# Decode attention with a gated output: the output in eight partitions of 112 columns, one store, and wo summed with two folds

## The chip, the core and the metric

The kernel runs on one core of one Trainium2 chip. The core has five engines with instruction queues of their own: TensorE (PE in the profile; its weight loads are listed as PEld), VectorE (DVE), ScalarE (ACT), GpSimd (POOL) and SyncE (SP). They share an on-chip memory of 128 partitions; TensorE writes its results into a second one, PSUM. Sixteen DMA engines move data between it and the device memory; SP and ACT issue transfers to them here. The metric is the device time of one execution in microseconds.

## The reference

The kernel computes one decode step for a batch of two: a layer norm of x, sliding-window attention over the last 2,048 positions of a cache, and a gate from a two-layer network.

```python
# B=2, Sq=1, D=448, Hq=16, Hkv=8, Dh=256, W=2048, Dff=1792; all bfloat16
xn = layernorm(x)                                   # (2, 1, 448)
q = xn @ wq                                         # 448 x 4096
scores = q . k_cache[:, :, Sk-W:, :] * Dh ** -0.5   # 16 heads, two per kv head
o = softmax(scores) . v_cache[:, :, Sk-W:, :]
s = o.reshape(2, 1, 4096) @ wo                      # 4096 x 448
g = silu(relu(xn @ w1) @ w2)
out = x + s * g
```

The caches count for 32 MiB of the loads, the four weight matrices for some 10 MiB more.

## The kernel before, in words

Every operation is put on a list of its engine (`_Prog.op`, `_Prog.dma`) with the operations that it depends on; the lists are emitted in the order in which they were written, with semaphore waits where a dependence crosses engines. So the order of the text is the order of each engine's queue. Nearly all matmuls go through the helper `mm` (line 241) and all transfers through line 35; in the profile they are told apart by their tiles.

SP loads wq, w1, w2, the four K tiles (4 MiB each, one for each batch element and group of four kv heads), then each V tile into the buffer of a K tile once that K tile's scores are done, and last wo in the six parts of `WO_PARTS`, into the buffer that wq had (`wqo`). wo lies with 32 rows j of 448 columns in every partition, so that a part is a range of j.

On TensorE, results of two rows (the batch) are common. To use more of the array, independent matmuls are put into different groups of 32 output columns (`tile_position`): four such groups (i or c times 32) run beside each other, and their results lie in partitions 0, 32, 64 and 96 of a PSUM bank. Where four groups hold partial sums of the same result, a fold adds them up: VectorE copies the bank into on-chip memory (f32), and a matmul with the matrix `f8` of ones sums the partitions 0, 32, 64 and 96.

`do_H` and `do_F` compute the gate early: h, then w2 in four groups into `fbk`, a copy `zc`, a fold into `mbk` in two groups of 224 columns (c = 0, 1, partitions 0 and 32), and the silu on 34 partitions (`ROWS`) by 224 columns (`NCOL`), into `g_sb`. The rows in between are not used.

The middle is the attention: `do_turn` transposes K on VectorE (line 276), `do_S` forms scores into `sbk`, `do_max`, `do_et`, `do_spread` and `do_pt` make the softmax, `do_PV` multiplies with V, `do_out` scales, and `do_turn_out` transposes the result into `at2`, the stationary operand of the wo product: for each j two columns, one of each batch element.

The end is what the change is about. wo's first part of 16 rows is multiplied in four groups into `wbk` (row j in group j mod 4), copied to `wc` (line 451) and folded into `fbk`, in two groups of 224 columns. The other sixteen rows go straight to `fbk` by `direct` (line 453): for each j two matmuls of 224 columns, c = 0 into partitions 0 and 1, c = 1 into 32 and 33. `fill` puts in matmuls whose results nobody reads, between the waits for wo. After the last row VectorE multiplies `fbk` with `g_sb` (line 474) and adds `x_c` (line 476), a copy of x in the same layout, which two small transfers on ACT's queue loaded at the start into memory that POOL had set to zero. Two stores, one on SP's and one on ACT's queue (line 478), write the halves, and each engine waits for its own.

Of the kernel before, what the change touches and what calls it, by code (L numbers as in the profile page):

```python
# [74 lines left out]
def bass_recurrent_scan__sliding_block_cached__dense_activation_relu__decode_kernel(  # L75
# [26 lines left out]
    NCOL = D // 2  # L102
    ROWS = 34
    WO_PARTS = [16, 4, 4, 4, 2, 2]
    WO_TILED = 16

    es = contextlib.ExitStack()
    with es:
# [35 lines left out]
        wc = named("wc", [128, D], F32)  # L144
        ea = named("ea", [128, NCOL], F32)
# [14 lines left out]
        at2 = named("at2", [128, 32 * 2], BF)  # L160
# [19 lines left out]
        p_xc = pr.op(POOL, lambda e: e.memset(x_c[:, :], 0.0))  # L180
        d_xc = [pr.dma(ACTE, x_c[32 * c:32 * c + B, :], A_x[:, 0, NCOL * c:NCOL * c + NCOL], [p_xc]) for c in range(2)]
# [6 lines left out]
        st = {}  # L188
# [3 lines left out]
        for u in range(NU):  # L192
# [7 lines left out]
               for t in (asel, rm, bt, qstat, at2)][-1]  # L200
# [24 lines left out]
        v_f8 = pr.op(DVE, red(f8[:, :], view(ident, 0, [[1, 8], [8, 16]])))  # L225
        v_h2 = pr.op(DVE, red(half2[:, :], view(ident, 0, [[8, 2], [16, 8], [1, 8]]), AX.XY))
# [133 lines left out]
        def do_turn_out(hg):  # L360
            if hg:
                fill(2)
            deps = [st["osb", 2 + hg], v_as, st["mbk"]]
            lo = 64 * hg
            for dq in range(8):
                o = pr.op(PE, mm(mbk[lo:lo + 64, 288:352], asel[:, 7 - dq:71 - dq],
                                 view(o_sb, hg * 2 * DH + 32 * dq, [[DH, B], [1, 32]]),
                                 dq == 0, dq == 7, tile_position=(0, lo)), deps)
                deps = []
            st["at"] = st["mbk"] = pr.op(DVE, lambda e: e.tensor_copy(  # L370
                view(at2, 0, [[1, B], [B, 32]], n=64, p0=lo), view(mbk, 288, [[32, B], [1, 32]], n=64, p0=lo)), [o, p_z])
# [15 lines left out]
        def do_F():  # L387
# [7 lines left out]
            deps = [v, v_f8, st["mbk"]]  # L395
            for c in range(2):
                o = pr.op(PE, mm(mbk[32 * c:32 * c + B, 0:NCOL], f8[:, 0:B], zc[:, NCOL * c:NCOL * c + NCOL],
                                 True, True, tile_position=(0, 32 * c)), deps)
                deps = []
# [46 lines left out]
        for j in range(WO_TILED):  # L446
            i = j % 4
            o = pr.op(PE, mm(wbk[32 * i:32 * i + B, 0:D], at2[:, B * j:B * j + B], wqo[:, j * D:j * D + D],
# [15 lines left out]
        deps = [v_wc]  # L464
        for c in range(2):
            pr.op(PE, mm(fbk[32 * c:32 * c + B, 0:NCOL], f8[:, 0:B], wc[:, NCOL * c:NCOL * c + NCOL], False,
                         tile_position=(0, 32 * c)), deps)
            deps = []
        for j in range(20, 32):
            if j in (20, 24):  # L470
                fill(1)
            m_o = direct(j, [landed.get(j)])
# [4 lines left out]
            out=out_sb[0:ROWS, :], in0=tmp[0:ROWS, :], in1=x_c[0:ROWS, :], op=ALU.add), [v_t] + d_xc)  # L477
# [33 lines left out]
```

## Time and profile before

| | us |
|---|---|
| median of three runs | 110.72 (110.68 to 110.85) |
| the profiled execution | 110.67 |
| its span, first to last instruction | 109.3 |
| DVE busy | 62.2 |
| PE busy | 57.0 |
| the first wo matmul | 102.53 |
| the last wo matmuls | 106.79 to 107.14 |
| product and sum on VectorE | 107.19 to 107.99 |
| both stores issued | 108.02 |

The times inside the span count from its start. Busy times of engines overlap and don't add up to the span. The span does not hold what lies before the first and after the last instruction, 1.3 us in the profiled execution.

### The profile page before, as it was taken

How to read it: one execution, taken by the hardware profiler on the slowest of the kernel's cores; microseconds unless marked ns; L12 is line 12 of the kernel's file. 1: busy time of each engine (PE TensorE's matmuls, PEld its weight loads, DVE VectorE, ACT ScalarE, POOL GpSimd, SP SyncE). 2: the span in 40 equal slices, each digit the busy share in tenths (PEclk: the TensorE clock that was granted, in tenths of full speed). 3: DMA queues.
4: the chain of work that ended last, by engine and by line, in shares of the span. 5: the costliest groups of instructions: out<-in, count | busy, mean ns of one | idle time of the engine just before them, and what ended most of it. 6: DMA issues, size and time to landing. Idle time of an engine off the chain costs nothing.

```text
span 109.3 us, 1081 instructions
## 1 busy us (share of the span) xinstructions
PE 57.0 (52%) x458; PEld 14.5 (13%) x458; DVE 62.2 (57%) x83; ACT 9.1 (8%) x18; POOL 2.1 (2%) x12
## 2 busy tenths in 40 slices
PE   0010559430000079929952994499339555937791
PEld 0000114100000011001100120010023122413230
DVE  2920046445099979999999999930457333004102
ACT  3970000010000000002000200020110000000000
POOL 7000000000000000000000000000000000000000
PEclk9999999985555555999995569958995999999999
DMA  6899999999999999999999999999999899999940
GB/s 168 336 452 397 408 436 501 396 455 438 444 396 455 467 408 396 455 467 408 408 458 444 408 420 467 432 420 402 467 432 420 378 444 420 444 413 410 405 187 1
DMA packets 2616, 44.17 MB, mean 404 GB/s; under 512 B 306, under 2 KB 564, under 8 KB 948
## 3 DMA queue, kind: packets, MB, share of 16 engines
q1 hardware_dynamic: 2596, 44.11, 94.7%
q8 instruction: 3, 0.05, 0.2%
q14 instruction: 1, 0.01, 0.0%
q10 hardware_dynamic: 16, 0.00, 0.0%
HBM read 44.11 MB, written 0.00 MB: 403 GB/s over the span
## 4 chain that ended last, share of the span: by engine, by line
DMA 57%; DVE 28%; PE 7%; SPq 5%; issue 1%
DMA kv<-in_A_k_cache_dram 34%; DVE kv L276 24%; DMA wqo<-in_A_wo_dram 23%; PE sbk L241 7%; SPq L35 5%; DVE q_x L305 1%; DVE rm L293 1%; DVE rm_t L295 0%; DVE bias L299 0%; DVE bt L296 0%; DVE tmp L474 0%; DVE out_sb L476 0%; PE fbk L241 0%
## 5 line engine op out<-in xcount | busy, mean ns | idle before, releaser
L241 PE MATMUL sbk<-kv,qstat 128*8 128x512 bf16 x128 | 29.9, 1086 | 23.9 <-DVE kv L276 23.9
L276 DVE STREAM_TRANSPOSE kv<-kv 128x2048 f32<-128x2048 f32 x16 | 35.6, 2276 | 4.6 <-DMA kv<-in_A_k_cache_dram 4.6
L241 PE MATMUL obk<-kv,pt 128*16 128x512 bf16 x128 | 9.3, 435 | 4.8 <-DVE xg L356 2.4
L241 PEld LDWEIGHTS sbk<-kv,qstat 128*8 128x8 bf16 x128 | 4.0, 107 | 48.4 <-DVE kv L276 30.2
L353 DVE TENSOR_SCALAR o_odd<-obk,rs 128x256 f32<-128x256 f32 x4 | 1.9, 484 | 11.6 <-PE obk L241 11.6
L300 ACT ACTIVATE e_sb<-sbk,bias 128x512 bf16<-128x512 f32 x4 | 2.7, 687 | 52.6 <-DVE bias L299 52.6
L241 PE MATMUL qbk<-wqo,xr 128*4 128x512 bf16 x28 | 3.2, 626 | 5.7 <-DMA wqo<-in_A_wq_dram 5.7
L259 DVE TENSOR_SCALAR q_x<-qbk 128x512 bf16<-128x512 f32 x1 | 0.7, 691 | 8.7 <-PE qbk L241 8.7
L293 DVE TENSOR_REDUCE rm<-sbk 128x1 f32<-128x512 f32 x4 | 2.6, 662 | 4.7 <-PE sbk L241 4.7
L241 PE MATMUL sbk<-kv,ident 128*32 128x512 bf16 x19 | 5.1, 380 | 0.0
L241 PEld LDWEIGHTS obk<-kv,pt 128*16 128x16 bf16 x128 | 3.2, 97 | 10.1 <-issue 5.8
L305 DVE STREAM_TRANSPOSE q_x<-e_sb 128x512 bf16<-128x512 bf16 x4 | 2.8, 691 | 1.7 <-ACT e_sb L300 1.7
L241 PE MATMUL mbk<-ident,xg 2*128 2x2 bf16 x7 | 0.3, 163 | 6.0 <-DVE xg L234 6.0
L322 DVE TENSOR_TENSOR pt<-spk,pmask 128x512 bf16<-128x512 f32 x4 | 2.6, 684 | 0.7 <-PE spk L241 0.7
L241 PE MATMUL qbk<-w_sb,xr 128*2 128x448 bf16 x28 | 2.8, 572 | 0.0
L241 PE MATMUL fbk<-wqo,at 128*2 128x224 bf16 x32 | 2.5, 258 | 0.4 <-DMA wqo<-in_A_wo_dram 0.4
L241 PE MATMUL spk<-q_x,perm 128*32 128x128 bf16 x16 | 0.6, 292 | 3.1 <-DVE q_x L305 3.1
L474 DVE TENSOR_TENSOR tmp<-fbk,g_sb 34x224 f32<-34x224 f32 x1 | 0.4, 383 | 3.1 <-PE fbk L241 3.1
L270 DVE CAST qstat<-mbk 32x256 bf16<-32x256 f32 x4 | 1.7, 421 | 0.7 <-PE mbk L241 0.7
L356 DVE SCALAR_TENSOR_TENSOR xg<-obk,rs,o_odd 128x256 bf16<-128x256 f32 x4 | 1.9, 484 | 0.1
L451 DVE COPY wc<-wbk 128x448 f32<-128x448 f32 x1 | 0.6, 625 | 2.4 <-PE wbk L241 2.4
L241 PEld LDWEIGHTS sbk<-kv,ident 128*32 128x32 bf16 x19 | 1.8, 97 | 1.8
(70 smaller groups left out, 33.1 us busy)
## 6 DMA issues: line engine op xcount, KB each, us to landing
kv<-in_A_k_cache_dram SPq DMA_DIRECT2D x4, 4096.0 KB, 41.3
kv<-in_A_v_cache_dram SPq DMA_DIRECT2D x3, 4096.0 KB, 22.1
kv<-in_A_v_cache_dram SPq DMA_DIRECT2D x2, 2048.0 KB, 18.0
wqo<-in_A_wq_dram SPq DMA_DIRECT2D x1, 3584.0 KB, 11.3
w_sb<-in_B_w_dram SPq DMA_DIRECT2D x2, 1568.0 KB, 16.2
wqo<-in_A_wo_dram SPq DMA_DIRECT2D x1, 1792.0 KB, 23.7
wqo<-in_A_wo_dram SPq DMA_DIRECT2D x3, 448.0 KB, 24.8
wqo<-in_A_wo_dram SPq DMA_DIRECT2D x2, 224.0 KB, 25.5
```

The costliest lines, as they stand in the source:

```text
L35: o = _Op(eng, lambda e: e.dma_start(dst, src), [d for d in deps if d is not None], True)
L241: return lambda e: e.matmul(out_ap, lhsT=lhsT, rhs=rhs, start=start, stop=stop, skip_group_check=True, **kw)
L259: v_q = pr.op(DVE, lambda e: e.tensor_scalar(out=view(q_x, 0, [[256, 8], [128, 2], [1, 32]]), in0=view(qbk, 0, [[64, 8], [1, 2], [2, 32]]) ...
L270: st["q"] = st["mbk"] = pr.op(DVE, lambda e, Q=Q: e.tensor_copy(qstat[32 * Q:32 * Q + 32, 256 * Q:256 * Q + 256], mbk[32 * Q:32 * Q + 32, ...
L276: st["turn", u] = pr.op(DVE, lambda e, n=n: e.transpose(kf[:, 2048 * n:2048 * n + 2048], kf[:, 2048 * n:2048 * n + 2048]), [d_k[u]])
L293: v = pr.op(DVE, lambda e: e.tensor_reduce(out=rm[:, 0:1], in_=sbk[u % 2][:, :], axis=AX.X, op=ALU.max), [last_S[u], p_z, st.get(("rmt", u ...
L300: st["exp", u] = pr.op(ACTE, lambda e: e.activation(e_sb[:, :], sbk[u % 2][:, :], ACT.Exp, bias=bias[:, 0:1], accum_out=ssum[:, u:u + 1]), ...
L305: st["et", u] = pr.op(DVE, lambda e: e.transpose(q_x[:, 512 * u:512 * u + 512], e_sb[:, :]), [st["exp", u], m_qt])
L322: st["pt", u] = pr.op(DVE, lambda e: e.tensor_tensor(out=view(pt[u], 0, [[8, 64], [2, 4], [1, 2]]), in0=view(spk, 128 * u, [[2, 64], [0, 4 ...
L353: v = pr.op(DVE, lambda e: e.tensor_scalar(out=o_odd[:, :], in0=obk[:, DH:2 * DH], scalar1=rs[:, 2 * u + 1:2 * u + 2], scalar2=None, op0=A ...
L356: st["osb", u] = pr.op(DVE, lambda e: e.scalar_tensor_tensor(out=o_sb[:, lo:lo + DH], in0=obk[:, 0:DH], scalar=rs[:, 2 * u:2 * u + 1], in1 ...
L451: v_wc = pr.op(DVE, lambda e: e.tensor_copy(wc[:, :], wbk[:, 0:D]), [o])
```

## The change

The layout of the output changes. It was two pieces (c = 0, 1) of 224 columns, each of two rows at partitions 32c and 32c + 1. It becomes eight adjacent partitions of 112 columns: partition 4b + c holds quarter c of batch element b, which is the order of the output in device memory. x is loaded so by one transfer (`x_c`), and ACT stores the output with one.

A matmul that shall write quarter c into rows 4b + c of eight, and add nothing to the others, takes a stationary operand of eight columns that is zero but for columns c and 4 + c. For this `at2` gets 11 columns for each j, zeros but for columns 3 and 7, and the slice of eight that begins at 3 - c has the two values at c and 4 + c. `fpad` is the same of `f8`, for the gate's fold: four matmuls in sequence into `mbk` rows 0 to 7. These slices have no `tile_position`.

wo comes in five parts (20, 4, 4, 2, 2 rows). Rows 0 to 23 are summed in four groups into `wbk` and folded once, into four groups by quarters in `sbk[1]`; rows 24 to 27 are added there in four groups of 112 columns. VectorE copies that bank (`qc`), and a second fold with `sel8` adds it to `fbk`, rows 0 to 7, in which rows 28 to 31 are summed by padded slices, four matmuls a row. In TensorE's order the second fold stands between rows 29 and 30. Three fills stand ahead of the first fold; the single fills between the later rows are gone. The diff, cut to its core:

```diff
-    NCOL = D // 2
-    ROWS = 34
-    WO_PARTS = [16, 4, 4, 4, 2, 2]
-    WO_TILED = 16
+    NCOL = D // 4
+    ROWS = 8
+    PADW = 11
+    WO_PARTS = [20, 4, 4, 2, 2]
+    WO_TILED = 24
+    WO_QUART = 28
...
-        p_xc = pr.op(POOL, lambda e: e.memset(x_c[:, :], 0.0))
-        d_xc = [pr.dma(ACTE, x_c[32 * c:32 * c + B, :], A_x[:, 0, NCOL * c:NCOL * c + NCOL], [p_xc]) for c in range(2)]
+        d_xc = pr.dma(ACTE, x_c[0:ROWS, :], A_x.rearrange("b s (c n) -> (b s c) n", c=4))
...
-               for t in (asel, rm, bt, qstat, at2)][-1]
+               for t in (fpad, asel, rm, bt, qstat, at2)][-1]
...
+        v_fp = pr.op(DVE, lambda e: e.tensor_copy(view(fpad, 3, [[4, B]]), f8[:, 0:B]), [v_f8, p_z])
+        v_s8 = pr.op(DVE, lambda e: e.tensor_copy(
+            view(sel8, 0, [[4, B], [1, 4]]), view(ident, 0, [[1, B], [32, 4]])), [p_id])
...
-                view(at2, 0, [[1, B], [B, 32]], n=64, p0=lo), view(mbk, 288, [[32, B], [1, 32]], n=64, p0=lo)), [o, p_z])
+                view(at2, 3, [[4, B], [PADW, 32]], n=64, p0=lo), view(mbk, 288, [[32, B], [1, 32]], n=64, p0=lo)), [o, p_z])
...
-            deps = [v, v_f8, st["mbk"]]
-            for c in range(2):
-                o = pr.op(PE, mm(mbk[32 * c:32 * c + B, 0:NCOL], f8[:, 0:B], zc[:, NCOL * c:NCOL * c + NCOL],
-                                 True, True, tile_position=(0, 32 * c)), deps)
+            deps = [v, v_fp, st["mbk"]]
+            for c in range(4):
+                o = pr.op(PE, mm(mbk[0:ROWS, 0:NCOL], fpad[:, 3 - c:3 - c + ROWS], zc[:, NCOL * c:NCOL * c + NCOL],
+                                 c == 0, c == 3), deps)
...
-            o = pr.op(PE, mm(wbk[32 * i:32 * i + B, 0:D], at2[:, B * j:B * j + B], wqo[:, j * D:j * D + D],
+            o = pr.op(PE, mm(wbk[32 * i:32 * i + B, 0:D], view(at2, PADW * j + 3, [[4, B]]), wqo[:, j * D:j * D + D],
...
-        def direct(j, deps):
-            for c in range(2):
+        fill(3)
+        deps = [v_wc, st["exp", 3]]
+        for c in range(4):
+            pr.op(PE, mm(sbk[1][32 * c:32 * c + B, 0:NCOL], f8[:, 0:B], wc[:, NCOL * c:NCOL * c + NCOL],
+                         True, tile_position=(0, 32 * c)), deps)
+            deps = []
+        for j in range(WO_TILED, WO_QUART):
+            for c in range(4):
                 lo = j * D + c * NCOL
-                o = pr.op(PE, mm(fbk[32 * c:32 * c + B, 0:NCOL], at2[:, B * j:B * j + B], wqo[:, lo:lo + NCOL],
-                                 j == WO_TILED, j == 31, tile_position=(0, 32 * c)), deps)
-                deps = []
-            return o
-
-        for j in range(WO_TILED, 20):
-            direct(j, [landed.get(j), st["g"]])
-        fill(1)
-        deps = [v_wc]
-        for c in range(2):
-            pr.op(PE, mm(fbk[32 * c:32 * c + B, 0:NCOL], f8[:, 0:B], wc[:, NCOL * c:NCOL * c + NCOL], False,
-                         tile_position=(0, 32 * c)), deps)
-            deps = []
-        for j in range(20, 32):
-            if j in (20, 24):
-                fill(1)
-            m_o = direct(j, [landed.get(j)])
+                o = pr.op(PE, mm(sbk[1][32 * c:32 * c + B, 0:NCOL], view(at2, PADW * j + 3, [[4, B]]),
+                                 wqo[:, lo:lo + NCOL], False, j == WO_QUART - 1, tile_position=(0, 32 * c)),
+                          [landed.get(j)])
+        v_qc = pr.op(DVE, lambda e: e.tensor_copy(qc[:, :], sbk[1][:, 0:NCOL]), [o])
+        for j in range(WO_QUART, 32):
+            if j == 30:
+                pr.op(PE, mm(fbk[0:ROWS, 0:NCOL], sel8[:, :], qc[:, :], False), [v_qc, v_s8])
+            for c in range(4):
+                lo = j * D + c * NCOL
+                m_o = pr.op(PE, mm(fbk[0:ROWS, 0:NCOL], at2[:, PADW * j + 3 - c:PADW * j + 3 - c + ROWS],
+                                   wqo[:, lo:lo + NCOL], j == WO_QUART and c == 0, j == 31 and c == 3),
+                            [landed.get(j), st["g"]])
...
-        for c, eng in ((0, SP), (1, ACTE)):
-            d_o = pr.dma(eng, out[:, 0, NCOL * c:NCOL * c + NCOL], out_sb[32 * c:32 * c + B, :], [v_o])
-            pr.op(eng, None, [d_o])
+        d_o = pr.dma(ACTE, out.rearrange("b s (c n) -> (b s c) n", c=4), out_sb[0:ROWS, :], [v_o])
+        pr.op(ACTE, None, [d_o])
```

More of the change, by code (lines that the diff above doesn't have):

```diff
@@ L144, in bass_recurrent_scan__sliding_block_cached__dense_activation_relu__decode_kernel @@
         wc = named("wc", [128, D], F32)
+        qc = named("qc", [128, NCOL], F32)
+        sel8 = named("sel8", [128, 8], F32)
+        fpad = named("fpad", [128, PADW], F32)
         ea = named("ea", [128, NCOL], F32)
@@ L159, in bass_recurrent_scan__sliding_block_cached__dense_activation_relu__decode_kernel @@
         o_odd = named("o_odd", [128, DH], F32)
-        at2 = named("at2", [128, 32 * 2], BF)
+        at2 = named("at2", [128, 32 * PADW], BF)
         wqo = named("wqo", [128, 32 * D], BF)
@@ L476, in bass_recurrent_scan__sliding_block_cached__dense_activation_relu__decode_kernel @@
         v_o = pr.op(DVE, lambda e: e.tensor_tensor(
-            out=out_sb[0:ROWS, :], in0=tmp[0:ROWS, :], in1=x_c[0:ROWS, :], op=ALU.add), [v_t] + d_xc)
-        for c, eng in ((0, SP), (1, ACTE)):
-            d_o = pr.dma(eng, out[:, 0, NCOL * c:NCOL * c + NCOL], out_sb[32 * c:32 * c + B, :], [v_o])
-            pr.op(eng, None, [d_o])
+            out=out_sb[0:ROWS, :], in0=tmp[0:ROWS, :], in1=x_c[0:ROWS, :], op=ALU.add), [v_t, d_xc])
+        d_o = pr.dma(ACTE, out.rearrange("b s (c n) -> (b s c) n", c=4), out_sb[0:ROWS, :], [v_o])
+        pr.op(ACTE, None, [d_o])
         pr.run()
```

## The prediction

> **What bounds the kernel now.** I read the page of the profile first (the forty slices and the chain that ended last), then the timeline from 102 us to the end, then the table of windows over the same stretch, and last the waits of SP's queue.
>
> The page, with the slices of granted clock and of the DMA engines:
>
> ```profile
> span 109.3 us, 1081 instructions
> PEclk9999999985555555999995569958995999999999
> DMA  6899999999999999999999999999999899999940
> DMA 57%; DVE 28%; PE 7%; SPq 5%; issue 1%
> ```
>
> The sixteen DMA engines are nine tenths busy or more from the third slice to the 38th. Loading 44 MB sets the time until about 105 us. TensorE's clock is full in the last nine slices. No edit takes a byte out of the loads, so the change can only move what follows them.
>
> The timeline of the end (start, duration, engine, line, operation, tiles; in brackets the idle time before it and what ended it):
>
> ```profile
> 102.53 0.93 PE L241 MATMUL wbk<-wqo,at 128*2 128x448 bf16 x16 [0.76 <-DMA wqo<-in_A_wo_dram]
> 103.51 0.62 DVE L451 COPY wc<-wbk 128x448 f32<-128x448 f32 x1 [2.43 <-PE wbk L241]
> ...
> 104.19 0.55 PE L241 MATMUL fbk<-wc,f 128*2 128x224 f32 x4
> ...
> 105.71 0.88 PE L241 MATMUL fbk<-wqo,at 128*2 128x224 bf16 x12 [0.16 <-DMA wqo<-in_A_wo_dram]
> 106.23 0.09 PEld L241 LDWEIGHTS fbk<-wqo,at 128*2 128x2 bf16 x4 [0.24 <-DMA wqo<-in_A_wo_dram]
> 106.79 0.09 PEld L241 LDWEIGHTS fbk<-wqo,at 128*2 128x2 bf16 x4 [0.47 <-DMA wqo<-in_A_wo_dram]
> 106.79 0.35 PE L241 MATMUL fbk<-wqo,at 128*2 128x224 bf16 x4 [0.21 <-DMA wqo<-in_A_wo_dram]
> 107.19 0.38 DVE L474 TENSOR_TENSOR tmp<-fbk,g_sb 34x224 f32<-34x224 f32 x1 [3.06 <-PE fbk L241]
> 107.61 0.38 DVE L476 TENSOR_TENSOR out_sb<-tmp,x_c 34x224 bf16<-34x224 f32 x1
> 108.02 0.33 SPq L35 DMA_DIRECT2D out_dram<-out_sb  x1
> 108.02 0.26 ACTq L35 DMA_DIRECT2D out_dram<-out_sb  x1
> ```
>
> Each later piece of wo is waited for; the fold of the first sixteen rows (copy at 103.51, fold matmuls at 104.19) is done long before the last piece. So the path is: last landing, four matmuls, product, sum, store, wait.
>
> Windows (length, busy time by engine, clock, DMA share, GB/s) and SP's waits:
>
> ```profile
> 104.00:105.00 1.00, 1.00 (x15) 0.55 (x13) 0.14 (x1) 0.00 (x0) 0.00 (x0) 1.00 0.89 344
> 105.00:106.00 1.00, 0.84 (x15) 0.42 (x10) 0.00 (x0) 0.00 (x0) 0.00 (x0) 1.00 0.27 102
> 106.00:107.00 1.00, 0.79 (x14) 0.18 (x8) 0.00 (x0) 0.00 (x0) 0.00 (x0) 1.00 0.05 18
> ```
>
> ```profile
> SPq L65 <- DMA out_dram<-out_sb: 1.0, 1, 1.0
> ```
>
> The bulk is in by 105; three of the sixteen engines trail (0.27, then 0.05 of all DMA time) and the last landing hangs on the slowest. The store costs a microsecond of pure waiting, and it is SP that waits last.
>
> By the trace's records the six pieces of wo land at 102.40, 103.48, 104.58, 105.67, 106.19 and 106.75. The profiled execution took 110.67 us: 109.35 of span and 1.32 around it. That is 0.05 under the median of 110.72; the sum below goes against 110.67.
>
> **The change part by part.**
>
> *Start.* One load of x on ACT's queue (eight pieces of 224 bytes) in place of two, without the wait for POOL's memset of x_c (0.28 us, gone). POOL gets a memset of fpad (11 columns; the 32-column ones take 0.12) and at2 grows from 64 to 352 columns: between 0.15 (64 columns) and 0.95 (1024), about 0.4. DVE gets two small copies, 0.17 each by the 128x8 copy. They push xg and xr from 6.41 to about 6.75; the wq matmuls that need xr wait for their load until 12.06, so 5 us cover it. SP's queue is not passed by any of this. It issues one DMA less (0.43) at 79 us, and the pieces land some 24 us after issue: nothing.
>
> *The gate (do_F).* Four f32 slices in sequence in place of two side by side: the two take 188 ns between passes of 224 columns, so four of 112 columns need 4 x 2 x 94 = 0.75 instead of 0.38 us. DVE's four operations and the Exp get narrower. All ends near 26 us; the next DVE work waits for the first K until 30.05. Cover 3.8 us: nothing. (Without the cover it would cost 0.4 less the narrower operations, about nothing.) The wider at2 write after the transposes (0.23 at 100.85) has 2.4 us before the first piece now lands.
>
> *Five wo parts.* The first piece is now 20 rows and lands where the second did, 103.48, perhaps 0.04 sooner: in the DMA records a packet of 14,336 bytes takes 535 ns and one of 3,584 takes 140, and by the slope of these 17,920 bytes need 668 in place of 675, eight times per engine. A gain of 0 to 0.1 at every later landing; I take none. TensorE now idles from 101.8 to 103.6. It had 1.7 us without work before 98.22 and kept the full clock, so I cost this at nothing (a rival below).
>
> *The fold chain, new on the path.* Steps, with rows: twenty rows from 103.61 (the first piece's matmuls start 0.13 after landing) in five groups of four at 188 ns, to 104.55. Rows 20 to 23 land at 104.58, run at 104.62 and end after 0.35, at 104.97. The copy of wc: 105.02 plus 0.625 = 105.65 (the three fills end before that: 3 x 0.215 from 104.8). First fold at 105.70: two passes of 94 ns in four column groups, to 105.89. Rows 24 to 27 (landed 105.67): four groups of 49 ns, the last ending at 105.89 + 3 x 0.049 + 0.21 = 106.25. (49 ns is half the 95 between 224-column matmuls of one column group; 0.21 is their 258 less 47.) The copy qc at 106.30: the 448-column copy takes 625 and a 256-column one 421, so 112 columns take 0.27: 106.57. The sel8 matmul at 106.63, two passes of 94: to 106.82. Rows 28 and 29 (landed 106.19) fill TensorE from 106.23 to 106.62 in between. So the last piece, landed at 106.75 and usable at 106.79, starts at 106.82. The two chains meet within 0.03 us: **no slack is left**, and every tenth by which the fold chain is longer is a tenth at the end.
>
> *The last two rows.* Eight matmuls in one column group in place of four in two: before, 0.35 to the end; now 7 x 0.049 + 0.21 = 0.55. TensorE ends at 107.37 in place of 107.15: plus 0.22. The 49 is an interpolation between rows of one column group: pairs of 64-column loads and 64-column matmuls (mbk from xg) follow each other every 32 ns, 224-column ones every 95. Between 32 and 95 the cost of this step lies between 0.08 and 0.52; 112 columns by the line between them give 51.
>
> The Trainium skill (TensorE: Matmul & The Clock Gate, Back-to-back issue gap) says that in a stream of load-and-matmul pairs 128 columns cost about 81 ns a matmul, against 56 alone. By that rule both groups of eight would grow; the sum would stand at 111.0, and the 32 ns of the row above speaks against it.
>
> *DVE's end.* Product and sum on 112 columns: 383 for 224 and 187 for 28 columns in the same operation give 1.0 ns a column, so 0.27 each in place of 0.38: minus 0.23. Product 107.41 to 107.68, sum 107.71 to 107.98, store issued at 108.01 in place of 108.02. Nothing gained, nothing lost.
>
> *The store.* Before, ACT's own store was complete for its wait at 109.16 by the trace's records, 1.14 us after issue; SP's, issued at the same time, at 109.33, 1.31 after. SP's packets start just behind ACT's (108.81 against 108.77) and take 0.50 from packet to semaphore against 0.36. Now only ACT stores, and the kernel ends with it. Floor: ACT's 1.14 again. Ceiling: two packets of one store start 0.02 apart, so six more one after another add 0.12; and neighbouring small writes may cost the 0.14 that SP's did: 1.40. No row of before shows eight pieces; I take the middle, 1.27: ready at 109.28 against 109.33.
>
> The Trainium skill (DMA: Bandwidth & Descriptors, Why a DMA increments its semaphore by 16 and not by 1) says that a DMA from such a queue spreads over the largest number of engines up to 16 that divides the slowest dimension on both sides. By it two rows use two engines and eight use eight, side by side; the sum would then be nearer its floor, 110.5. No run so far shows where eight pieces go.
>
> Sum: start 0, gate 0, landings 0, last part + 0.22, DVE - 0.23 (with the 0.03 of the fold chain inside), store - 0.04 to - 0.05: about - 0.06, or **110.6 us**, 0.1 below the median. A measurement of this kernel tells about 0.2% (0.22 us) from no change, so this reads as no change.
>
> **The rivals.**
>
> *The store's end is the gain (faster).* If ACT's 1.14 holds for eight pieces, the span ends 0.18 sooner; with 0.04 to 0.1 from earlier landings and a fold chain no longer than worked out, 110.67 - 0.18 - 0.07 = 110.4. For it: SP is the last to wait today. Against: eight pieces are smaller and touch each other in memory.
>
> *Padded slices run slower than their columns (slower).* Place: the sixteen matmuls of rows 28 to 31, where each loads new weights into the column group that the one before uses. From 75 ns on in place of 49, rows 28 and 29 end at 106.83, sel8 at 107.02, the last eight end at 107.02 + 7 x 0.075 + 0.21 = 107.76: 0.39 later than in the sum, 111.0. It decides from about 68 ns a matmul. Against it: 32 ns per pair with 64 weights, and some 26 ns per pair with 128 weights and 16 columns (sixteen in 0.59).
>
> *The double fold binds.* If the copy, the f32 passes or the wait for the second landing is longer than worked out by 0.3, the last part starts 0.3 late: 110.9. The same place loses 0.9 (seven short PE steps from 104.6 on, 0.9 us of streaming, at half rate) if the longer idle before 103.6 drops the clock: 111.5. Against: each step is from a row, and the clock held through a similar gap.
>
> *Small writes are slow.* If pieces that share a stretch of memory wait for one another more than once, 0.14 each time: three times gives 1.14 + 0.12 + 0.42 = 1.68, or 111.0. For it: SP's slower acknowledgement. Against: that may be SP's place behind ACT's packets.
>
> **How the numbers follow.** The forecast, with all ends between 110.5 and 110.9: 0.53. Store gain: 0.27, around 110.4. Slow slices 0.08; double fold or clock 0.06; slow small writes 0.06; these three lie at 110.9 to 111.5. Faster 0.27, same 0.53, slower 0.20. Range 110.3 to 111.0: from the store gain with the largest landing gain to the slow slices; the clock and a part of the others are left out. The likeliest case's own range is 110.5 to 110.9.
>
> **What would show it.** In the profile after: no wait for DMA ahead of wc's first matmuls other than at about 103.5; a wc copy ending near 105.65 and a qc copy of about 0.27 ending near 106.6; eight matmuls in about 0.55 after the last landing; two DVE operations of 0.27; an issue on ACT near 108.0, and 1.1 to 1.4 us to the end. The prediction is wrong if the qc copy or sel8 is what the last matmuls wait for by a tenth or more, if the eight take over 0.7, if the clock is below full after 103, or if the last landing moves by more than 0.1 for reasons of the loads, which nothing in the change explains.

## The result and the profile after

The changed kernel took 112.12 us, the median of six runs (111.63 to 113.01), against 110.73 before (110.39 to 110.92, six runs): a ratio of 1.0133, with a 95% interval of 1.0087 to 1.018. I had forecast 110.6 in a range of 110.3 to 111.0. It became 1.4 us slower, and the time lies outside my range. A ratio is formed from the executions within 1.5% of the kernel's fastest and a median from all of them; in the table of the experiments three executions of e5 and two each of e9 and e15 lie above that and count in the median alone.

The page of the profile after (the second line is the granted clock of TensorE in forty slices, the third the share of the DMA engines, the fourth the queue that fetches instructions, the fifth the chain that ended last):

```profile
span 110.7 us, 1116 instructions
...
PEclk9999999998555555996695589859976999999999
DMA  6798999999999899989989999999999899999910
...
q8 instruction: 4, 0.07, 0.2%
...
DMA 56%; DVE 28%; PE 10%; SPq 3%; issue 1%
```

The loads still set the time, and TensorE's clock is full at the end of this execution. The fetch queue has four packets where the kernel before had three.

The timeline of the end (start, duration, engine, line, operation, tiles; in brackets the idle time before it):

```profile
103.82 1.46 PE L248 MATMUL wbk<-wqo,at 128*2 128x448 bf16 x24 [1.89 <-DMA wqo<-in_A_wo_dram]
...
105.33 0.62 DVE L458 COPY wc<-wbk 128x448 f32<-128x448 f32 x1 [3.88 <-PE wbk L248]
...
106.54 0.56 PE L248 MATMUL fbk<-wqo,at 128*8 128x112 bf16 x8
106.62 0.28 DVE L471 COPY qc<-sbk 128x112 f32<-128x112 f32 x1 [0.67 <-PE sbk L248]
...
106.95 0.36 PE L248 MATMUL fbk<-qc,sel 128*8 128x112 f32 x2
...
107.14 0.56 PE L248 MATMUL fbk<-wqo,at 128*8 128x112 bf16 x8
107.74 0.26 DVE L481 TENSOR_TENSOR tmp<-fbk,g_sb 8x112 f32<-8x112 f32 x1 [0.84 <-PE fbk L248]
108.04 0.26 DVE L483 TENSOR_TENSOR out_sb<-tmp,x_c 8x112 bf16<-8x112 f32 x1
108.33 0.30 ACTq L35 DMA_DIRECT2D out_dram<-out_sb  x1
```

The durations are the ones I had worked out: the copy `qc` takes 0.28, eight padded matmuls 0.56, the two operations on VectorE 0.26 each. But all of it is 0.3 us late. By the trace's records the last piece of wo lands at 107.06 (106.75 before), and the store is issued at 108.33, where I had 108.01. The last report of the store then comes 2.34 us after its issue, where I had 1.27 (before, 1.29): the span ends at 110.7.

The windows of the end, in the columns of those of before, show the loads running longer: 0.34 and 0.10 of the DMA time in the last two, against 0.27 and 0.05.

```profile
104.00:105.00 1.00, 1.00 (x24) 0.38 (x17) 0.00 (x0) 0.00 (x0) 0.00 (x0) 1.00 1.00 375
105.00:106.00 1.00, 0.91 (x7) 0.21 (x5) 0.62 (x1) 0.00 (x0) 0.00 (x0) 1.00 0.34 126
106.00:107.00 1.00, 0.99 (x33) 0.84 (x34) 0.28 (x1) 0.00 (x0) 0.00 (x0) 1.00 0.10 38
```

What the store met is in the view of the DMA queues, from 108.5 us to the end (the first line is the share of the engines in forty slices, the others are queue, packets, MB and share):

```profile
DMA  0900000000100000000000000000000000000000
...
q8 instruction: 1, 0.02, 2.3%
q10 hardware_dynamic: 16, 0.00, 0.5%
```

The nine in the second slice is an instruction fetch of 16 KB, which by the records starts at 108.62 and takes 0.94 us on one of the sixteen engines. The store has eight packets of 224 bytes; by their overlapping starts and the eight reports I take them to be on eight engines. Seven start at 109.11 to 109.17 and are reported at 109.45 to 109.53. The eighth starts at 109.55, just as the fetch ends, and is reported at 110.67, 1.14 us after the others; I read it as the one on the fetch's engine. So in this execution the 1.51 us against the profiled execution of before (112.18 against 110.67) are 0.31 at the issue of the store, 1.05 in the store and 0.15 outside the span.

### The profile page after: what moved, and what is told of

Its sections match the earlier page's. It is cut to its first block, busy times and chain, and to the rows that moved or that the text cites. A ratio compares the mean times of both kernels' runs of the same rounds, so it can differ in the third digit from the quotient of the medians.

```text
span 110.7 us, 1116 instructions
## 1 busy us (share of the span) xinstructions
PE 57.0 (51%) x476; PEld 15.9 (14%) x476; DVE 62.0 (56%) x86; ACT 9.0 (8%) x18; POOL 2.2 (2%) x12
## 4 chain that ended last, share of the span: by engine, by line
DMA 56%; DVE 28%; PE 10%; SPq 3%; issue 1%
DMA kv<-in_A_k_cache_dram 34%; DVE kv L283 24%; DMA wqo<-in_A_wo_dram 22%; PE sbk L248 7%; SPq L35 3%; PE wbk L248 1%; DVE q_x L312 1%; DVE rm L300 1%; PE fbk L248 1%; DVE wc L458 1%; DVE rm_t L302 0%; DVE bias L306 0%; DVE bt L303 0%; DVE tmp L481 0%; DVE out_sb L483 0%
## 5 line engine op out<-in xcount | busy, mean ns | idle before, releaser
L248 PE MATMUL wbk<-wqo,at 128*2 128x448 bf16 x24 | 1.5, 352 | 1.9 <-DMA wqo<-in_A_wo_dram 1.9
L248 PE MATMUL mbk<-xg,asel 128*64 128x64 bf16 x16 | 0.9, 199 | 1.8 <-DVE xg L363 1.8
```

What stands on the lines that cost most here:

```text
L248: return lambda e: e.matmul(out_ap, lhsT=lhsT, rhs=rhs, start=start, stop=stop, skip_group_check=True, **kw)
```

## The experiments

Four groups of runs, each with the kernel before beside it. All but three (e4, e13 and e14, one execution each) were run several times. "Last landing", "clock" and "fetch" are of the one profiled execution: the time at which the last piece of wo had landed, whether the clock was halved while TensorE worked after 101 us, and the start of the last instruction fetch after 100 us, where there is one.

| kernel | us, median (range) | before | ratio (95% interval) | last landing | clock | fetch |
|---|---|---|---|---|---|---|
| after | 112.12 (111.63 to 113.01) | 110.73 | 1.0133 (1.0087 to 1.018) | 107.06 | full | 108.62 |
| e1: after, 20 matmuls fewer | 111.56 (111.14 to 112.57) | 110.64 | 1.0091 (1.0047 to 1.0134) | 107.08 | halved | none |
| e2: before, 20 matmuls more | 110.80 (110.32 to 111.34) | 110.64 | 1.001 (0.9987 to 1.0033) | 106.75 | full | none |
| e3: after, 40 matmuls more | 111.41 (111.0 to 112.53) | 110.64 | 1.0073 (1.0038 to 1.0107) | 107.72 | full | 106.85 |
| e5: after, 32 bytes | 112.38 (111.11 to 113.99) | 110.64 | 1.0113 (1.0069 to 1.0157) | 107.12 | full | none |
| e6: before, 32 bytes | 111.49 (111.22 to 111.96) | 110.64 | 1.0064 (1.0031 to 1.0098) | 107.71 | full | none |
| e7: after, eight fills | 111.48 (111.11 to 111.88) | 110.64 | 1.0072 (1.0048 to 1.0095) | 107.22 | full | 107.73 |
| e8: after, e5, e7 and e3 | 111.52 (111.19 to 111.74) | 110.64 | 1.0067 (1.0045 to 1.0089) | 107.20 | full | 105.59 |
| e9: after, 160 bytes | 111.10 (110.4 to 112.28) | 110.68 | 1.0022 (0.9992 to 1.0051) | 106.40 | full | none |
| e10: e9, eight fills | 110.70 (110.51 to 111.46) | 110.68 | 1.0009 (0.9986 to 1.0031) | 107.41 | full | 108.10 |
| e11: e10, store on SP | 110.72 (110.31 to 111.25) | 110.68 | 0.9996 (0.9978 to 1.0014) | 106.59 | full | 106.92 |
| e12: before, 256 bytes | 110.70 (110.41 to 111.21) | 110.68 | 1.001 (0.9991 to 1.0029) | 106.50 | full | none |
| e13: after again, one execution | 112.25 | 110.59 | | 107.05 | halved | none |
| e14: after a third time, one execution | 112.09 | 110.59 | | 107.00 | halved | none |
| e15: e9, 40 matmuls more | 111.2 (110.47 to 112.31) | 110.59 | 1.0034 (1.0005 to 1.0062) | 106.54 | halved | 105.20 |

### The fetch at the store (e1 to e4)

The first theory was that the fourth fetch is the loss: the kernel after has more TensorE instructions, and a fetch comes due at the store. e1 takes 20 matmuls out of the hidden layer of the gate (which is then summed over two of its seven slices only), e2 gives the kernel before 20 tiny matmuls, e3 gives 40 to the kernel after, and e4 is the kernel before, once more.

```diff
 # e1, in do_H
-            for s in range(SLOTS):
+            for s in (0, SLOTS - 1):
 # e2 (range(20), in before) and e3 (range(40), in after), behind do_F()
+        for _ in range(20):
+            pr.op(PE, mm(wbk[0:2, 0:16], ident[:, 0:2], ident[:, 0:16], True, True), [z(wbk), p_id])
```

> The changed kernel with 20 matmuls fewer early on (the hidden layer of the gate is summed over two of its seven slices only, so the gate is another one): TensorE's stream is 923 records long, under the 927 of the kernel before, in place of 963. Fetch theory (the store of the changed kernel waits for a fourth 16 KB instruction fetch that starts at 108.6 us on one of the eight DMA engines that carry the store): three fetches, the store complete 1.1 to 1.25 us after its issue in place of 2.36, time 110.9 to 111.1 if the last landing stays 0.3 us later, 110.6 if it doesn't. Small-pieces theory (eight pieces of 224 bytes are slow to be acknowledged): still some 2.3 us from issue to completion, time 111.7 to 112.3.

> The kernel before with 20 tiny matmuls (two rows by 16 columns, result not read) behind the gate, in TensorE's long wait at 24 us: its stream grows from 927 to 967 records. Fetch theory: a fourth 16 KB fetch appears near the end, at about 108.3 to 108.9 us; the two stores use few engines, so with a chance of about one in eight to one in two it holds one of them up by about a microsecond (time 111.7 to 112), otherwise time 110.6 to 110.9. Small-pieces theory: nothing, 110.5 to 110.9, whatever is fetched.

> The changed kernel with 40 such tiny matmuls behind the gate: 1043 records. Fetch theory: the fourth fetch is asked for 80 records sooner and so starts at 106 to 107.8 us, between the last landing and the store; the store is complete 1.1 to 1.4 us after its issue, time 110.7 to 111.2. If the fetch meets the last piece of wo on a late engine the landing moves by up to 0.6 us and the time is 111.3 to 111.6. Small-pieces theory: 111.7 to 112.3 as the changed kernel.

> The kernel before once more, for its scatter from one execution to the next. If the changed kernel's last landing (107.06 us against 106.75) is scatter, this one lies anywhere from 106.5 to 107.2; if it is a matter of the loads, it lies within 0.05 of 106.75.

e1 has three fetches and e3 has its fourth earlier, at 106.85. In both, the eight packets of the store start together and the span ends 1.2 us after the issue (e1: issue 109.29, span 110.5). So the store alone costs 1.2 us, inside my 1.14 to 1.40, and what held it in the profile after was, by the times above, the fetch. Yet e1 and e3 were still slower than before by 0.9 and 0.8 us, so the fetch is not all. e3's last landing (107.72) is later still: the last of the sixteen reports of that piece trails the one before by 0.68 us, and the records do not show why. e2 missed: with 478 matmuls by its profile, against 476 in the kernel after, no fourth fetch is in its profile. What exactly brings the fetch on is not settled by these runs. One more execution of the kernel before (e4, 110.68) had its last landing at 106.74, so that time repeats.

e1's profile showed a second thing. Its windows, cut at the times where the granted clock changed (columns as above; the last but two is the clock):

```profile
99.59:103.00 3.41, 1.67 (x14) 0.64 (x12) 1.30 (x3) 0.00 (x0) 0.00 (x0) 1.00 0.96 402
103.01:106.42 3.41, 2.59 (x25) 0.97 (x26) 0.13 (x1) 0.00 (x0) 0.00 (x0) 0.50 0.73 278
```

The clock was halved for 3.41 us, just as the first 24 rows of wo ran; they took 2.41 us in place of 1.46. And a third: the last landing, 107.08, was as late as in the kernel after, with no fetch near.

### Where the load buffers begin, and the idle TensorE (e5 to e8)

In the compiled kernel the new tensors, and the ones that were halved, move the buffers that the loads write. `wqo` begins at byte 43,264 of each partition before and at 42,592 after, the first K buffer at 97,024 and 96,352. The first of each pair is a multiple of 256, the second is not (it leaves 96). In the records of before, every one of the 256 packets of 1,792 bytes takes 74 ns; after, 129 of them take longer, up to 87, and packets of 32 KB take 1,218.9 ns in the mean in place of 1,214.6. (The mean for 32 KB is no sure sign: e4, the kernel before with its buffers where they were, has 1,217.2.) Summed up and divided by sixteen, the packets of a whole execution take 103.87 us in place of 103.56, and the last landing is later by the same 0.31.

e5 puts 32 bytes ahead of `wqo` in the kernel after, which makes the starts multiples of 64 and 128; e6 puts the same 32 bytes into the kernel before, which takes its starts off the multiples of 64. e7 doubles the fills ahead of the wo product. e8 has the gap of e5, the fills of e7 and the tiny matmuls of e3.

```diff
 # e5 (in after) and e6 (in before), ahead of wqo
+        gap32 = named("gap32", [128, 8], F32)
 # e7, ahead of the wo product
-        fill(4)
+        fill(8)
```

> The changed kernel with an unused tensor of 32 bytes ahead of wqo, so that wqo and all that lies behind it (w1, w2, the K and V buffers) begin again at a multiple of 64 bytes, as before; in the changed kernel they begin 32 bytes past one (kv0 at 96,352 in place of 97,024). Address theory (the loads of the changed kernel end 0.3 us late because their packets into such buffers are now and then slower: the 1,792-byte packet took 74 to 87 ns in place of 74 throughout): all 1,792-byte packets at 74 ns, last landing 106.7 to 106.8, the time 0.3 us under the changed kernel's, 111.6 to 111.9. Scatter theory (this is the state of the memory, not of the kernel): 107.0 to 107.1 again, 112.0 to 112.2. The fourth fetch and the clock are as they were, so it stays above 111 on both.

> The kernel before with the same unused 32 bytes, which moves its buffers off the multiple of 64. Address theory: packets of 1,792 bytes between 74 and 87 ns, last landing at 107.0 to 107.1 in place of 106.75, time 110.9 to 111.1. Scatter theory: 106.75 and 110.6.

> The changed kernel with eight fills in place of four ahead of the wo product, so that TensorE idles 0.9 us less before the first part of wo lands. Clock theory (in some executions the idle from 101.9 to 103.8 us drops the clock to half for 3.4 us, which made the first wo matmuls 0.96 us longer in one profile): the spans lose their upper group; highest time at most 112.2 in place of 113.0 (the fetch is still there), median 111.4 to 111.7. Without that theory: as the changed kernel, 112.1, highest 112.6 to 113.

> The changed kernel with the 32 bytes, the eight fills and 40 tiny matmuls early, which move the fourth fetch ahead of the store. If the three causes (fetch behind the store, addresses, clock) are all there is: last landing 106.7 to 106.8, no slow clock after 102, the store complete 1.2 us after issue at 108.0, time 110.5 to 110.8 with a spread as narrow as before's (0.7 us). If something else costs (a store on ACT alone that ends the kernel later, outside the span): 110.8 to 111.1.

e6 is the proof of the addresses: 32 unused bytes, and no other edit, make the kernel before 0.85 us slower (111.49 against 110.64). 160 of its 1,792-byte packets are slow. The timeline of its end (lines are one further down than in before):

```profile
103.29 0.93 PE L242 MATMUL wbk<-wqo,at 128*2 128x448 bf16 x16 [0.86 <-DMA wqo<-in_A_wo_dram]
...
107.76 0.36 PE L242 MATMUL fbk<-wqo,at 128*2 128x224 bf16 x4 [0.20 <-DMA wqo<-in_A_wo_dram]
...
108.98 0.32 SPq L35 DMA_DIRECT2D out_dram<-out_sb  x1
```

The first part of wo starts 0.76 us later than in before (103.29 against 102.53), the last four matmuls 0.97 (107.76 against 106.79); the tail behind them has its old length. The packets account for a part of it: their sum over sixteen is 104.09 us here, 0.53 over before.

e5 missed: a multiple of 64 or 128 bytes isn't enough. 107 packets stay slow, the last landing is at 107.12, and the time (112.38) is no better than after. So the boundary that counts here is wider than 128 bytes. e8 missed too, since it was built on e5's boundary: 111.52.

e7 takes 0.64 us off the kernel after and brings its spread from 1.38 down to 0.77. Its own profile does not show the part of the fills, because the attention happened to end late in it (the work ahead of the wo product would have ended at 103.3 with four fills too, as in e5). In e8 it ended early, at 101.1, and there the eight fills take 1.90 us in place of 1.04; TensorE idles 1.02 us ahead of the wo product in place of 1.89, and the window has 2.39 us of work and keeps the clock:

```profile
101.46:104.87 3.41, 2.39 (x27) 0.90 (x25) 0.16 (x1) 0.00 (x0) 0.00 (x0) 1.00 0.96 379
```

The four fills more also move the fourth fetch forward, to 107.73; it ends at 109.03, before the store's packets start at 109.25. So e7 changes two things at once, the idle time and the fetch at the store, and its 0.64 us can't be divided between them: e3, which moves the fetch and keeps four fills, has as low a median (111.41), and e8, which does both, has 111.52. What the fills do show is at the top: spans reach 111.1 in e3 and 110.2 in e8. Nor is the store of e7's profile free of the fetch. Seven of its reports come by 109.67 and the eighth at 110.20, 1.74 us after the issue and 1.18 after the end of the fetch; in the profile after the late report came 1.12 us after the fetch's end.

### Multiples of 256 (e9 to e12)

e9 puts 160 bytes ahead of `wqo` in the kernel after (starts at 42,752 and 96,512, multiples of 256), e10 adds the eight fills, e11 also stores on SP's queue, and e12 is the kernel before moved by 256 bytes, as a control.

```diff
 # e9, e10, e11 (in after); [128, 64] in e12 (in before)
+        gap = named("gap", [128, 40], F32)
 # e10, e11
-        fill(4)
+        fill(8)
 # e11
-        d_o = pr.dma(ACTE, out.rearrange("b s (c n) -> (b s c) n", c=4), out_sb[0:ROWS, :], [v_o])
-        pr.op(ACTE, None, [d_o])
+        d_o = pr.dma(SP, out.rearrange("b s (c n) -> (b s c) n", c=4), out_sb[0:ROWS, :], [v_o])
+        pr.op(SP, None, [d_o])
```

> The changed kernel with 160 unused bytes ahead of wqo, which puts wqo, w1, w2 and the K and V buffers at multiples of 256 bytes (wqo at 42,752, kv0 at 96,512), as in the kernel before (43,264 and 97,024); with the gap of 32 bytes wqo was at a multiple of 64 and 128 but not of 256, and the packets stayed slow. Address theory, now with 256: every 1,792-byte packet 74 ns, last landing 106.7 to 106.8 (the changed kernel 107.06, with the 32-byte gap 107.13). Theory that something else in the changed kernel disturbs the loads: 107.0 to 107.2 and packets up to 87 ns again. Fetch and clock are left, so the spread stays wide: 110.9 to 112.8, median 111.3 to 111.8.

> The same gap and eight fills ahead of the wo product. With eight fills the fourth fetch came at 107.7 and was done before the store, and the spread was 0.8 us. If addresses, clock and fetch are all three mended: landing 106.75, store issued at 108.0, complete 1.2 later, span 109.2 to 109.4, and 1.47 outside the span as in the other runs whose store is ACT's: 110.6 to 110.9. If the addresses don't matter in this kernel: 111.4 to 111.6 as with eight fills alone.

> As e10, with the one store on SP's queue in place of ACT's. The time outside the span is 1.31 (median) in the runs of before, which SP's wait ends, and 1.47 where ACT's wait is the last. If that is due to the engine which ends the kernel: 0.1 to 0.2 under e10, 110.4 to 110.7. If not: the same as e10 within 0.1.

> The kernel before with 256 unused bytes ahead of wqo: everything is moved, but by a whole 256. Address theory: 1,792-byte packets at 74 ns, landing 106.7 to 106.8, 110.5 to 110.8, no difference from before. If any shift of the buffers costs (32 bytes cost 0.85 us): 111.2 to 111.6.

In all four every packet of 1,792 bytes takes 74 ns again. e12 is no other than before, so it is not the moving that costs, but where the buffers begin. e9 takes 1.02 us off the kernel after. The end of its profiled execution, which was its fastest (110.4):

```profile
103.27 1.35 PE L249 MATMUL wbk<-wqo,at 128*2 128x448 bf16 x24 [1.82 <-DMA wqo<-in_A_wo_dram]
...
106.50 0.56 PE L249 MATMUL fbk<-wqo,at 128*8 128x112 bf16 x8
...
107.68 0.29 ACTq L35 DMA_DIRECT2D out_dram<-out_sb  x1
```

and the end of the control, the kernel before moved by 256 bytes:

```profile
106.54 0.36 PE L242 MATMUL fbk<-wqo,at 128*2 128x224 bf16 x4 [0.20 <-DMA wqo<-in_A_wo_dram]
...
107.77 0.32 SPq L35 DMA_DIRECT2D out_dram<-out_sb  x1
```

With the loads undisturbed the new end issues its store as early as the old one. e9 still goes up to 112.28, and its idle 1.82 us ahead of the wo product is still there; two of its longest three (111.92 and 112.2) have spans of 109.5 and 109.6 only and lose their time outside (last section). e10, with the eight fills, is the same as before (1.0009, interval 0.9986 to 1.0031). From e7 to e10 only the addresses differ: 0.78 us, which agrees with the 0.85 of e6. e10's profiled execution was its longest (110.0 of span): the last landing is at 107.41, because the last of the sixteen reports trailed the one before by 0.55 us. The records do not name the engine, and why it trailed is not shown. In e11, with the store on SP's queue, the time is the same as in e10.

### What remains with four fills (e13 to e15)

Two more executions of the kernel after, and e9 with the forty tiny matmuls of e3, which move the fourth fetch away from the store and leave the fills at four.

> The kernel after once more, one look. If the fourth instruction fetch belongs to this program's stream, its records show one again, starting between 107.5 and 109.5 us, and where it begins before the store's packets and runs on the engine of one of them, the store takes over 2 us from issue; where it begins elsewhere or on one of the other eight engines, 1.2 us. If the fetch in the first profile was chance, no fourth one is seen. In both cases the packets of 1,792 bytes are slow (mean over 75.5 ns, as the addresses are the same) and the last piece of wo lands at 107.0 to 107.5.

> The same kernel a third time, for the same reason: how the place and the engine of the fourth fetch vary from one execution to the next. Time between 111.1 and 113.0: 111.1 to 111.5 where neither the store is held nor the clock drops, 1.1 more where the store is held, up to 1 more where the clock drops.

> The addresses at multiples of 256 bytes and forty tiny matmuls early, with four fills as in the kernel after. If the fourth fetch at the store is a part of what is left in the kernel with the addresses alone (111.10), it moves to 105 to 107 us here, and the times lie at 110.5 to 111.0, with a top below 111.6. If what is left there is the clock alone, the forty matmuls change nothing: 111.0 to 111.2, with a top above 112, and eight fills (110.70) were all that it needed. Packets of 1,792 bytes all 74 ns in both cases; last landing 106.4 to 106.8 unless an engine that had two fetches trails.

The two executions took 112.25 and 112.09, as long as the first profile (112.18), and by another way: there is no fourth fetch in either span, the store takes 1.2 us, and the clock is halved. e14's timeline:

```profile
103.76 2.41 PE L248 MATMUL wbk<-wqo,at 128*2 128x448 bf16 x24 [1.89 <-DMA wqo<-in_A_wo_dram]
...
108.19 0.56 PE L248 MATMUL fbk<-wqo,at 128*8 128x112 bf16 x8
...
109.38 0.30 ACTq L35 DMA_DIRECT2D out_dram<-out_sb  x1
```

Its last piece lands at 107.00, sooner than in the first profile, but the first 24 rows take 2.41 us, and the last eight matmuls start 1.05 us later than there. Its windows, cut where the clock changed:

```profile
100.03:103.44 3.41, 1.41 (x12) 0.64 (x12) 0.82 (x2) 0.00 (x0) 0.00 (x0) 1.00 0.95 390
103.44:106.86 3.42, 3.10 (x27) 1.13 (x27) 0.62 (x1) 0.00 (x0) 0.00 (x0) 0.50 0.58 218
```

and the same of e13, where the window lies 1.65 us later:

```profile
101.68:105.09 3.41, 1.52 (x27) 0.54 (x26) 0.00 (x0) 0.00 (x0) 0.00 (x0) 1.00 0.98 384
105.10:108.51 3.41, 3.41 (x45) 2.46 (x41) 0.90 (x2) 0.00 (x0) 0.00 (x0) 0.50 0.11 41
```

For comparison the window of the kernel before that holds its first wo matmuls, and that of the first profile of the kernel after, in that order:

```profile
102.12:105.53 3.41, 2.94 (x39) 1.38 (x39) 0.62 (x1) 0.00 (x0) 0.00 (x0) 1.00 0.87 345
```

```profile
102.11:105.52 3.41, 1.70 (x26) 0.72 (x27) 0.19 (x1) 0.00 (x0) 0.00 (x0) 1.00 0.91 353
```

The kernel before has 2.94 us of work in this stretch. The kernel after has 1.41, 1.52 and 1.70 in its three profiles, by where the window falls. After the first two the next 3.41 us ran at half the clock, after the third they did not.

My expectation of a fourth fetch in both executions was a miss. e15 went the way of the second theory in its expectation: with the fetch at 105.20, out of the way, its median (111.2) and its top (112.31) are those of e9. Its profiled execution (110.1 of span) has the halved clock again, behind a window with 1.71 us of work. So the clock is a part of what is left with the addresses right, and the eight fills of e10 take it away: no span of e10 and e11 is over 110.0 (24 executions), six of 22 are in e9 and e15, up to 110.8. In the middle it is worth less. The medians fall by 0.4 us from e9 and 0.5 from e15, but a part of e9's is outside the span, and by the ratios, which leave the longest executions out, e9 and e15 are 0.2% and 0.3% slower than before and e10 0.1%, with intervals that overlap.

Three profiles of the same kernel thus end at 110.7, 110.8 and 110.6, one through the store and two through the clock. In all three the parts of wo land late, the last at 107.0 to 107.1; where the clock was halved it is the fold chain that the last matmuls wait for, and no longer this landing.

## Why the prediction was wrong

The sum for the change's own steps holds: e10, which has all of them and the gap and four fills besides, takes 110.70 us, and I had 110.6. Three things that the change brings with it make most of the 1.4 us, and each has a step in my prediction where it should have stood; a fourth, outside the span, I can't explain.

*Five wo parts.* I took the landings over from before ("I take none"), and wrote that nothing in the change explains a landing that moves by more than 0.1. This step failed first. The new tensors moved every large load buffer off a multiple of 256 bytes, and the loads that end at 106.75 before end at 107.0 to 107.1 after (the changed kernel with its buffers put right has 106.4 to 106.6 in e9, e11 and e15). That is worth 0.85 us by e6 and 0.78 from e7 to e10. I never asked where the buffers lie. The code shows nine tensors that are new or change size (`qc`, `sel8`, `fpad`, `at2` and the five of `NCOL` columns), so the question was there to be asked; the trace of before, where every packet of a size takes the same time, could not show the cost.

*The idle TensorE.* In the same part I costed the 1.8 us of idle time at nothing, because TensorE "had 1.7 us without work before 98.22 and kept the full clock". The mechanism was the right one and stood among the rivals, with a loss of 0.9, near the 1.05 us that e14 shows between the last eight matmuls of two profiles; but I put it at a few per cent (0.06 for it and the binding fold together), and it was in two of three profiles. What failed was the reading: I compared the length of two gaps. What counts is the work in a whole window of 3.41 us, whose position differs from one execution to the next. The stretch before 98.22 lay in a window with 1.73 us of work and was just enough. A stretch with 1.4 to 1.7 is not safe, and that is what the window near 102 has in all three profiles of the kernel after, in e1, in e9 and in e15. (In e3 and e5, also with four fills, it has 2.6 to 3.1: in e5 the work ahead of it ended later, at 103.3 instead of 101.9.)

*The store.* Its own time was right: 1.21 to 1.25 us in nine profiles of the changed kernel (e1, e3, e5, e8 to e10 and e13 to e15), between my floor of 1.14 and the ceiling of 1.40, so the rival of slow small writes falls. But my ceiling took the DMA engines to be free by then. The kernel after has a fourth instruction fetch within reach of the store, and in one of three profiles it held one of the eight packets for 1.14 us. In e7 and e11 one report came 0.53 and 0.38 us after the others, 1.18 us after the end of a fetch that had run before the store's packets started; I read this as the same cause, which the records, without the engines' names, don't prove. The share of this in the median can't be given alone. Taking it away with the clock left as it is lowers the kernel after by 0.7 us (e3) and the one with aligned buffers not at all (e15 against e9), and between executions with and without a halved clock such medians move by half a microsecond.

*The sum outside the span.* I set this equal. It is 1.44 to 1.52 us in most executions of the kernels that store on ACT and 1.28 to 1.38 in e11, which stores on SP, as in before. So the 0.08 that the store gains inside the span (1.21 against 1.29) is lost outside it. e11's spans are longer by as much (109.4 against 109.2 in the median) and its total is that of e10; as one report of its profiled store is late, it stays open whether the queue alone would gain something. And three of the six timed executions of the kernel after have 1.79 to 2.41 us here: a part of its median for which no run shows the cause.

*What was right.* The wider at2, the gate and the start cost nothing. The fold chain took the times I gave, and "no slack is left" is exact: in the profile after the last piece lands at 107.06, the second fold's last pass starts at 107.05 and takes some 95 ns, to 107.14, and the last eight matmuls start at 107.145. The padded slices follow each other every 49 ns, as interpolated, so that rival falls. At the full clock the last matmuls start right behind the second fold in every profile, but only 0.02 to 0.09 us later than the landing alone would have let them (0.04 after it, as in before), so the double fold hardly binds; with the halved clock it does, since they start at 108.19 there. The store gain, my likeliest way to a faster kernel, did not show: e10 and e11 are level with before.

In the medians: eight fills alone (with the fetch that they move) take off 0.64 us, the addresses alone 1.02, both 1.42, and 1.39 is the whole loss. The parts do not add up one by one, and the medians of all executions contain the time outside the span. No kernel here is faster than the kernel before.

## What to carry to other kernels

Before a new tensor is added to a kernel that loads decide, look at where its load buffers begin, and compare the packet times of a size in both traces: 32 bytes cost more here than the whole tail that was being rewritten could gain. Judge an idle stretch of TensorE by the work in the 3.4 us around it, in its worst placement, and not by its length. One profile shows one execution: where times of the same kernel spread by 1%, take two or three profiles before a cause is named, since here the first showed the store and the next two the clock.

## What the runs showed of the hardware

*The clock follows the work in windows of 3.41 us.* In every profile the granted clock changes only at multiples of 3.413 us from each other, and the start of this grid differs between executions. The record of the clock begins 15 to 45 us into the span. I took all windows of the 17 profiles that ran at the full clock from there on, and TensorE's busy time in each. Of those with less than 1.5 us of matmuls, 63 of 63 were followed by half the clock; from 1.5 to 1.7, 13 of 17; from 1.7 to 2.0, 9 of 36; above, 2 of 135. The turn is near half of the window. The Trainium skill (TensorE: Matmul & The Clock Gate, What's actually happening) describes a free-running window of 3,413 ns, and the traces agree. It gives an idle window as what throttles the clock; here windows with 1.5 to 1.7 us of work mostly did so too, and the measurement decides.

*Load buffers that don't begin at a multiple of 256 bytes make the loads slower.* The effect is small in a packet (74 to 76.5 ns in the mean for 1,792 bytes, 140 to 142.1 for 3,584, 1,214.6 to 1,218.9 for 32 KB) and is seen from about 34 us on in the kernel after and from 26 in e6; the packets of wq, w1 and w2 ahead of that take their old times, though their buffers lie off the multiples too. The Trainium skill (DMA: Bandwidth & Descriptors, How a descriptor splits into AXI transactions) says that a descriptor (one piece of a transfer) that starts off a multiple of 256 bytes costs additional beats on the bus; it speaks of what is read, and here the side that is written was moved. The runs agree on 256, since 128 (e5) wasn't enough. Why the first loads are spared is open.

*An instruction fetch occupies one of the engines that carry the data.* It takes 0.9 to 1.4 us, and a store of eight small packets waits for the slowest. The Trainium skill (Runtime: NRT & Kernel Launch, Instruction fetch mechanics) calls the cost of such a block mostly hidden; in the first profile of the kernel after the last packet of the store was reported 1.14 us behind the others.

*Some executions had 0.2 to 1.2 us more outside the span.* Against some 1.5 us as a rule, 1.66 to 2.69 appeared in 3 of 8 executions of the kernel after, 3 of 10 of e5 and 2 of 10 of e9; e2, where the rule is 1.3, had 1.57, 1.63 and 2.24 in 3 of 10; and it appeared in none of the 61 of e1, e3, e7, e8, e10 and e15. The first four have 476 to 478 matmuls by their profiles. Of the others e1 has 456 and no fourth fetch, and the rest have 480 or more and their fourth fetch at 108.1 or sooner. A fetch that is still running when the program ends would fit, but no record shows it.
